# Gate rows and output of the text tokens merged into one 32-column tiled run, text adds moved to GpSimd, first P copy moved to VectorE

## The chip, the cores and the metric

The kernel runs on one core of one Trainium2 chip. A core has TensorE (matrix products into the accumulator memory PSUM), VectorE, ScalarE and GpSimd for elementwise work, and DMA queues that are issued from SyncE (SP), ScalarE (ACT) and GpSimd (POOL). In the profile they are PE (with PEld for the loading of a product's stationary operand), DVE, ACT, POOL and SP. The time is the device's time of one execution in microseconds (us); a kernel's time is the median of several.

## The reference

One attention block in which image and text tokens attend jointly. Batch B is 2, with 256 image tokens and 32 text tokens each, width D = 1152; all inputs are bfloat16.

```python
mod_i = (_silu(c) @ wmod_img).reshape(B, 6, 1, D)
mod_t = (_silu(c) @ wmod_txt).reshape(B, 6, 1, D)
shi, sci, gai = mod_i[:, 0], mod_i[:, 1], mod_i[:, 2]
sht, sct, gat = mod_t[:, 0], mod_t[:, 1], mod_t[:, 2]
hi = _layernorm(x_img) * (1 + sci) + shi
ht = _layernorm(x_txt) * (1 + sct) + sht
qkvi, qkvt = hi @ wqkv_img, ht @ wqkv_txt
q, k, v = (concatenate([text part, image part], axis=1) for each third)
p = softmax(einsum('bqd,bkd->bqk', q, k) * D ** (-0.5))
a = einsum('bqk,bkd->bqd', p, v)
at, ai = a[:, :Nt], a[:, Nt:]
out_i = x_img + gai * (ai @ wo_img)
out_t = x_txt + gat * (at @ wo_txt)
```

The change touches the probabilities p, the text gate gat and the text output out_t.

## The kernel before

Width D is cut into KT = 9 row blocks of 128. All products go through the helper `mm` (line 61), transposes through `tr` (line 64); both pin their instruction into program order on TensorE with `pin` (`tc.keep_in_program_order`, line 58). VectorE and ScalarE instructions that are not pinned are placed by the tile scheduler. Every PSUM tile comes from one of two pools: `ps_mm` (six buffers) and `ps_tr` (two buffers, lines 55 and 56). The pool `work` (line 53) has two buffers per tag; the tag "tmp" holds an output product before the residual is added.

Weights lie in five large slots (`wtile`, line 76) that are reused. They are all loaded from the SP queue, one after the other, in the order of the calls; a load waits until the last reader of its slot is done. The end of that order is lines 566 to 571: text key weights, image gate weights, text value weights, image output weights `w_o_i`, text gate weights `w_ga_t`, and last the text output weights `w_o_t`. `load_rows` (line 93) cuts a load into pieces of whole row blocks; `w_o_t` comes in blocks 0 to 4 and 5 to 8. It takes the slot of the text value weights, so its load is issued when `v_txt(1)` (line 696) has read them.

The end of the kernel, in TensorE's order:

1. Scores and softmax (lines 672 to 693), the image gate rows, and the text values `v_txt` (line 505). `v_txt` and `mod_rows` (line 525) use a narrow form: TensorE is cut into four strips of 32 columns, `tile_position=(0, 32 * g)`, and four products run side by side.
2. The transposed probabilities: `p_transposes` (line 630) makes three PSUM tiles, one per block of keys; `p_out` (line 638) copies them to pT in SBUF, in halves for the two batch elements.
3. Attention, `attn_pair` (line 657), three times; the first products read the first half of the first P tile.
4. `out_img(i, ...)` (line 708) for the four image token tiles of 128 tokens. A tile is done in column chunks of CH = 384 (the last tile in 384, 384, 224 and 160): nine products of 128x128 by 128x384 fill a PSUM tile, VectorE multiplies it by the image gate `gb` into a tmp buffer (line 721), adds the input x_i (line 722), and a DMA stores the row.
5. `txt_gate` (line 556) is called by `out_img(1)` after its first chunk. `mod_rows` makes the 36 gate products, ScalarE copies them (line 535), and GpSimd's queue writes the two batch rows to a scratch in memory (line 537) and reads them back spread over the token partitions into `gbf` (line 561), four DMAs.
6. `out_txt` (line 728) stands between `out_img(2)` and `out_img(3)`. The 64 text tokens of both batch elements are one stationary operand of 64 columns; two products run side by side in two 64-column strips. Two PSUM tiles (r = 0, 1), 18 products each; VectorE multiplies each by gbf (line 738) and adds the text input xf (line 739); two stores go out on the SP and ACT queues.

Of the kernel before, what the change touches and what calls it, by code (L numbers as in the profile page):

```python
# [14 lines left out]
def kernel(  # L15
# [14 lines left out]
    nc = tc.nc  # L30
    bf = mybir.dt.bfloat16
    f32 = mybir.dt.float32
    PSUM = bass.MemoryType.PSUM

    B, NI, D = x_img.shape
    NT = x_txt.shape[1]
    P = 128
    KT = D // P
# [3 lines left out]
    NTT = B * NT  # L42
    CH = 384
    NCH = D // CH
    VC = 288
# [9 lines left out]
    ps_mm = ctx.enter_context(tc.tile_pool(name="ps_mm", bufs=6, space=PSUM))  # L55
    ps_tr = ctx.enter_context(tc.tile_pool(name="ps_tr", bufs=2, space=PSUM))

    pin = tc.keep_in_program_order

    def mm(*a, **k):  # L60
        return pin(nc.tensor.matmul(*a, **k))  # L61

    def tr(*a, **k):
        return pin(nc.tensor.transpose(*a, **k))  # L64
# [6 lines left out]
    x_i = act.tile([P, NIT, D], bf)  # L71
# [4 lines left out]
    def wtile(slot):  # L76
        return wpool.tile([P, KT, D], bf, tag="w%d" % slot, name="t")

    def wview(src, c0):
        return src.rearrange("(kt p) n -> p kt n", p=P)[:, :, c0:c0 + D]  # L80
# [3 lines left out]
    def load_w(slot, src, c0, splits=(D,)):  # L84
        t = wtile(slot)
        sv = wview(src, c0)
        o = 0
        for n in splits:
            nc.sync.dma_start(t[:, :, o:o + n], sv[:, :, o:o + n])
            o += n  # L90
        return t

    def load_rows(slot, src, c0, cuts=(0, 3, 6)):
        t = wtile(slot)
        sv = wview(src, c0)
        for r0, r1 in zip(cuts, cuts[1:] + (KT,)):
            nc.sync.dma_start(t[:, r0:r1, :], sv[:, r0:r1, :])
        return t
# [147 lines left out]
    def x_tiles(k0, b):  # L246
        return (tp61 if b else tp60) if k0 == 6 else ps_tr.tile([P, 3, NI], bf, tag="tr", name="tp")
# [70 lines left out]
    t3, t0, t6 = [(x_tiles(k0, 1), k0, 1) for k0 in (3, 0, 6)]  # L318
# [63 lines left out]
    def qk_img(wq, blk, hooks):  # L382
        for j in range(KT):
            for hook in hooks.get(j, ()):
                hook()
            ps = ps_mm.tile([P, B * NI], f32, tag="mm")
            for kt in range(KT):
                mm(ps[:], lhsT=wq[:, kt, j * P:(j + 1) * P], rhs=hT_i[:, kt, :],
                   start=(kt == 0), stop=(kt == KT - 1))
            qk_evac(qkT[:, blk * KT + j, :, 0:NI], ps[:].rearrange("p (b n) -> p b n", b=B), blk)  # L390
# [51 lines left out]
    def shift_part(r0, r1):  # L442
        def run():
            for kt in range(r0, r1):
                for b in range(B):
                    acc, col = acc_sh[:, b, :], sTf[:, kt, b:b + 1]
                    if kt == 0:
                        pin(nc.vector.tensor_scalar(acc, w_sh_t[:, kt, :], col, None, op0=ALU.mult))
                    else:
                        pin(nc.vector.scalar_tensor_tensor(acc, w_sh_t[:, kt, :], col, acc,  # L450
                                                           op0=ALU.mult, op1=ALU.add))
        return run
# [62 lines left out]
    def v_txt_out(r, ps):  # L515
        pin(nc.vector.tensor_sub(v_t[:, r * VC:(r + 1) * VC], ps[:], svb[:, r * VC:(r + 1) * VC]))
        if r == 0:
            pin(nc.vector.tensor_sub(v_t[0:NTT, HD:HD + NTT], ps[NTT:P, 0:NTT], svb[NTT:P, 0:NTT]))
# [6 lines left out]
    def mod_rows(w_blk):  # L525
        gps = ps_mm.tile([P, VC], f32, tag="mm")
        for kt in range(KT):
            for g in range(NGG):
                mm(gps[32 * g:32 * g + 32, :], lhsT=sT32[:, kt, :], rhs=w_blk[:, kt, g * VC:(g + 1) * VC],
                   start=(kt == 0), stop=(kt == KT - 1), tile_position=(0, 32 * g))  # L530
        return gps

    def mod_row_out(gps, si):
        g_sb = work.tile([P, VC], bf, tag="garow")
        pin(nc.scalar.copy(g_sb[:], gps[:]))
        for b in range(B):
            nc.gpsimd.dma_start(gsc[si, b, :].rearrange("(g j) -> g j", g=NGG), g_sb[b:P:32, :])

    gb = act.tile([P, B, D], bf, tag="Bt")
    gbf = act.tile([P, 2, VC], bf)  # L540
    xf = act.tile([P, 2, VC], bf)
# [14 lines left out]
    def txt_gate():  # L556
        mod_row_out(mod_rows(w_ga_t), 1)
        for g in range(2):
            for b in range(B):
                r0 = 64 * g + 32 * b  # L560
                nc.gpsimd.dma_start(gbf[r0:r0 + NT, :, :],
                                    gsc[1, b, :].rearrange("(r g j) -> g r j", r=2, g=2)[g].partition_broadcast(NT))
# [5 lines left out]
    w_v_t = load_w(1, wqkv_txt, 2 * D)  # L568
    w_o_i = load_rows(4, wo_img, 0)
    w_ga_t = load_w(3, wmod_txt, 2 * D)  # L570
    w_o_t = load_rows(1, wo_txt, 0, (0, 5))
    qk_img(w_q_i, 0, {0: (shift_part(0, 2),), 3: (txt_stats, shift_part(2, 4), txt_var, txt_norm),
                      5: (shift_part(4, 7),), 8: (shift_part(7, KT),)})
    qk_img(w_k_i, 1, {1: (txt_transposes,), 4: (txt_rows_scale, shift_blocks, txt_scale),
# [3 lines left out]
    aT = act.tile([P, KT, B * NTOK], bf, tag="Q")  # L578
# [51 lines left out]
    def p_transposes(kj, pool):  # L630
        ps = pool.tile([P, B * NTOK], bf, tag="tr" if pool is ps_tr else "mm", name="pT_ps")
        k0 = kj * P
        for pb, c0, o in [(pbs[(0, qi)], k0, qpos[0][qi]) for qi in range(TPB)] + [(pbs["t"], k0, NI)] + \
                [(pbs[(1, qi)], k0 - (NT if kj == 2 else 0), NTOK + qpos[1][qi]) for qi in range(TPB)]:
            tr(ps[:, o:o + P], pb[:, c0:c0 + P], ident[:])
        return ps

    def p_out(kj, ps, copy, b0=0, b1=B):
        pin(copy(pT[:, kj, b0 * NTOK:b1 * NTOK], ps[:, b0 * NTOK:b1 * NTOK]))
# [55 lines left out]
    v_txt_out(0, vt[0])  # L695
    vt.append(v_txt(1))
    pt0, pt1, pt2 = p_transposes(0, ps_tr), p_transposes(1, ps_tr), p_transposes(2, ps_mm)
    v_txt_out(1, vt[1])
    p_out(0, pt0, nc.scalar.copy, 0, 1)
    p_out(0, pt0, nc.vector.tensor_copy, 1, B)  # L700
    p_out(1, pt1, nc.scalar.copy, 0, 1)
    p_out(2, pt2, nc.vector.tensor_copy)
    p_out(1, pt1, nc.scalar.copy, 1, B)
    img_gate_spread()
    for dts in ((0, 5, 1), (6, 2, 7), (3, 8, 4)):
        attn_pair(*[[(b, dt) for dt in dts] for b in range(B)])

    def out_img(i, chunks, parts=None, between=None):
        b = i // TPB
        t0 = b * NTOK + qpos[b][i % TPB]  # L710
        o = work.tile([P, D], bf, tag="o")
        c0 = s0 = 0
        for n in chunks:
            if c0 and between:
                between = between()
            ps = ps_mm.tile([P, CH], f32, tag="mm")
            for dt in range(KT):
                mm(ps[:, 0:n], lhsT=aT[:, dt, t0:t0 + P], rhs=w_o_i[:, dt, c0:c0 + n],
                   start=(dt == 0), stop=(dt == KT - 1))
            tmp = work.tile([P, CH], bf, tag="tmp")  # L720
            nc.vector.tensor_mul(tmp[:, 0:n], ps[:, 0:n], gb[:, b, c0:c0 + n])  # L721
            nc.vector.tensor_add(o[:, c0:c0 + n], tmp[:, 0:n], x_i[:, i, c0:c0 + n])  # L722
            c0 += n
            if parts is None and c0 == D or parts and c0 in parts:
                (nc.scalar if parts and c0 == D else nc.sync).dma_start(oi_v[b, i % TPB, :, s0:c0], o[:, s0:c0])
                s0 = c0

    def out_txt():
        of = work.tile([P, 2, VC], bf, tag="of", bufs=1)
        for r in range(2):  # L730
            ps = ps_mm.tile([P, VC], f32, tag="mm")
            for dt in range(KT):
                for g in range(2):
                    c0 = (2 * r + g) * VC
                    mm(ps[64 * g:64 * g + NTT, :], lhsT=aT[:, dt, NI:NI + NTT], rhs=w_o_t[:, dt, c0:c0 + VC],
                       start=(dt == 0), stop=(dt == KT - 1), tile_position=(0, 64 * g))
            tmp = work.tile([P, CH], bf, tag="tmp")
            nc.vector.tensor_mul(tmp[:, 0:VC], ps[:], gbf[:, r, :])
            nc.vector.tensor_add(of[:, r, :], tmp[:, 0:VC], xf[:, r, :])
        for g in range(2):  # L740
            eng = nc.sync if g == 0 else nc.scalar
            eng.dma_start(ot_flat.rearrange("t (r g j) -> g t r j", r=2, g=2)[g], of[64 * g:64 * g + NTT, :, :])

    C3 = (CH, CH, CH)
    out_img(0, C3)
    out_img(1, C3, between=txt_gate)
    out_img(2, C3)
    out_txt()
    out_img(3, (CH, CH, 224, 160), parts=(2 * CH, D - 160, D))


# [28 lines left out]
```

## Time and profile before

| | us |
|---|---|
| median of 5 runs (lowest, highest) | 117.51 (117.22, 117.61) |
| the profiled execution | 117.67 |
| its span, first to last instruction | 115.5 |
| TensorE busy | 109.8 |
| VectorE busy | 72.1 |
| ScalarE busy | 43.7 |
| GpSimd busy | 12.1 |
| mean DMA rate over the span | 355 GB/s |

The granted clock of TensorE is 1.0 throughout. The profile's timeline merges instructions of one line and one kind: a row has the start, the time covered, the engine, line, operation, tiles, the shapes, the count, and in brackets the idle time before with what ended it. "PEld" rows show when TensorE changes to other stationary operands; their starts mark the stages. SPq, ACTq and the POOL DMA rows are the issue of DMAs, and the landing is given apart. A duration of a TensorE product includes its pipeline; products that follow each other start closer together than that.

### The profile page before, as it was taken

The page shows a single profiled execution, that of the slowest core. Times are in us where ns is not written, and L with a number is a line of the kernel's source. Part 1 is how long each engine was busy: PE and PEld are TensorE (multiplying, and loading weights), DVE is VectorE, ACT ScalarE, POOL GpSimd, SP SyncE. Part 2 cuts the span into 40 slices and gives each one's busy share as a digit, 9 for nine tenths or more (in the row PEclk, how much of TensorE's full clock was granted, in tenths as well). Part 3 has the DMA queues.
Part 4 walks back from the last instruction along what each step waited for, and adds up shares of the span by engine and source line. Part 5 has one row for each costly group of instructions (what it writes and reads, how often), then busy time and mean ns, then how long its engine had stood idle before and what let it go on. Part 6 is the DMA issues. An engine that isn't in the chain of part 4 may idle for free.

```text
span 115.5 us, 2579 instructions
## 1 busy us (share of the span) xinstructions
PE 109.8 (95%) x1078; PEld 63.4 (55%) x1078; DVE 72.1 (62%) x152; ACT 43.7 (38%) x93; POOL 12.1 (11%) x32
## 2 busy tenths in 40 slices
PE   4988999999999999999999999999999999999990
PEld 2335644445574444445444458787866556656670
DVE  3569592063869999999996040018768509566571
ACT  5799700041752279825240324244647400100000
POOL 7200000000000000000000000002440700415000
PEclk9999999999999999999999999999999999999999
DMA  3999999999999999999999999999999999942223
GB/s 118 372 361 389 397 403 409 415 412 409 410 400 413 335 402 407 406 415 410 413 366 386 413 404 413 409 411 406 412 404 410 404 419 367 397 180 51 102 51 102
DMA packets 18917, 41.02 MB, mean 355 GB/s; under 512 B 1323, under 2 KB 1851, under 8 KB 18907
## 3 DMA queue, kind: packets, MB, share of 16 engines
q1 hardware_dynamic: 18032, 39.85, 89.8%
q0 software_dynamic: 480, 0.89, 2.4%
q10 hardware_dynamic: 395, 0.12, 0.4%
q8 instruction: 8, 0.13, 0.4%
q14 instruction: 2, 0.02, 0.0%
HBM read 39.52 MB, written 1.34 MB: 354 GB/s over the span
## 4 chain that ended last, share of the span: by engine, by line
PE 86%; ACT 5%; DMA 3%; DVE 3%; issue 1%; DVEq 0%
PE ps L61 53%; PE vps L61 15%; PE gps L61 5%; PE aps L61 5%; PE sps L61 4%; DMA x_i<-in_x_img_dram 3%; ACT xn_i L194 2%; ACT xn_i L195 2%; PE tp L64 1%; DVE tmp L721 1%; PE pT_ps L64 1%; PE sc_ps L61 1%; DVE o L722 1%; DVE xT_i L257 0%; DVE xn_i L209 0%
## 5 line engine op out<-in xcount | busy, mean ns | idle before, releaser
L61 PE MATMUL ps<-xT_i,t 128*128 128x512 bf16 x162 | 35.7, 379 | 0.0
L61 PEld LDWEIGHTS <-t 128*128 128x128 bf16 x333 | 21.0, 98 | 19.3 <-issue 0.7
L450 DVE SCALAR_TENSOR_TENSOR acc_sh<-t,sTf,acc_sh 128x1152 f32<-128x1152 bf16 x16 | 21.4, 1405 | 0.0
L61 PE MATMUL ps<-t,aT 128*128 128x384 bf16 (+3 forms) x153 | 20.3, 308 | 0.0
L61 PE MATMUL vps<-t,hS_i 128*128 128x512 bf16 (+1 forms) x108 | 17.9, 326 | 0.2 <-DVE hS_i L269 0.2
L61 PEld LDWEIGHTS <-aT 128*128 128x128 bf16 (+1 forms) x153 | 13.0, 101 | 7.1 <-issue 0.8
L61 PEld LDWEIGHTS <-hS_i 128*128 128x128 bf16 x108 | 9.1, 98 | 8.9 <-DVE hS_i L269 0.4
L721 DVE TENSOR_TENSOR tmp<-ps,gb 128x384 bf16<-128x384 f32 (+2 forms) x13 | 6.8, 525 | 7.8 <-PE ps L61 7.8
L380 ACT CAST qkT<-ps 128x512 bf16<-128x512 f32 (+2 forms) x11 | 6.1, 552 | 14.8 <-PE ps L61 13.5
L607 POOL TENSOR_SCALAR pb<-e,rs 128x32 bf16<-128x32 f32 (+1 forms) x5 | 2.3, 458 | 76.1 <-DVE rs L599 76.1
L378 ACT ACTIVATE qkT<-ps 128x512 bf16<-128x512 f32 (+2 forms) x11 | 5.9, 559 | 8.2 <-PE ps L61 8.2
L177 DVE CAST v_i<-vps 128x512 bf16<-128x512 f32 x5 | 3.5, 692 | 8.0 <-PE vps L61 8.0
L61 PE MATMUL wps<-warm 128*128 128x512 bf16 x24 | 7.0, 446 | 1.5 <-DVE unit L127 1.5
L587 DVE TENSOR_REDUCE nmx<-sps 128x1 f32<-128x288 f32 x4 | 1.8, 458 | 9.4 <-PE sps L61 9.4
L179 ACT CAST v_i<-vps 128x512 bf16<-128x512 f32 x4 | 2.3, 580 | 10.2 <-PE vps L61 10.2
L61 PEld LDWEIGHTS <-sT 128*32 128x32 bf16 x180 | 4.5, 96 | 1.8 <-issue 1.2
L61 PE MATMUL sps<-qkT 128*128 128x288 bf16 (+1 forms) x54 | 5.3, 287 | 0.0
L652 DVE TENSOR_SCALAR aT<-aps,svc 128x288 bf16<-128x288 f32 x9 | 4.3, 518 | 1.5 <-PE aps L61 1.5
L61 PE MATMUL gps<-t,sT 128*32 128x288 bf16 x144 | 5.2, 287 | 0.0
L61 PEld LDWEIGHTS <-warm 128*128 128x128 bf16 x25 | 2.6, 112 | 4.8 <-issue 1.9
L61 PE MATMUL aps<-pT,v_i 128*128 128x288 bf16 x36 | 5.1, 287 | 0.0
L61 PE MATMUL ps<-hT_t,t 128*128 128x64 bf16 x162 | 5.1, 193 | 0.0
(112 smaller groups left out, 104.8 us busy)
## 6 DMA issues: line engine op xcount, KB each, us to landing
t<-in_wqkv_txt_dram SPq DMA_DIRECT2D x3, 2592.0 KB, 19.5
t<-in_wmod_img_dram SPq DMA_DIRECT2D x2, 2592.0 KB, 14.4
t<-in_wmod_txt_dram SPq DMA_DIRECT2D x2, 2592.0 KB, 18.6
t<-in_wqkv_img_dram SPq DMA_DIRECT2D x3, 864.0 KB, 13.5
t<-in_wqkv_img_dram SPq DMA_DIRECT2D x1, 2592.0 KB
t<-in_wo_img_dram SPq DMA_DIRECT2D x3, 864.0 KB, 10.3
t<-in_wqkv_img_dram SPq DMA_DIRECT2D x3, 576.0 KB, 10.9
t<-in_wmod_txt_dram SPq DMA_DIRECT2D x2, 864.0 KB, 13.2
```

The costliest lines, as they stand in the source:

```text
L61: return pin(nc.tensor.matmul(*a, **k))
L64: return pin(nc.tensor.transpose(*a, **k))
L177: nc.vector.tensor_copy(out_ap, in_ap)
L179: nc.scalar.copy(out_ap, in_ap)
L194: pin(nc.scalar.activation(junk, x_ap, ACT.Copy, scale=1.0 / D, accum_out=sm[:, 0:1]))
L195: pin(nc.scalar.activation(junk, x_ap, ACT.Square, scale=float(D) ** -0.5, accum_out=sm[:, 1:2]))
L378: nc.scalar.mul(out_ap, in_ap, SCALE)
L380: nc.scalar.copy(out_ap, in_ap)
L450: pin(nc.vector.scalar_tensor_tensor(acc, w_sh_t[:, kt, :], col, acc, op0=ALU.mult, op1=ALU.add))
L607: pin(nc.gpsimd.tensor_scalar(dst, src, rs[0:qn, :], 0.0, op0=ALU.mult, op1=ALU.add))
L652: nc.vector.tensor_scalar(dst, tiles[(b, dt)][:], bias, None, op0=ALU.add)
L721: nc.vector.tensor_mul(tmp[:, 0:n], ps[:, 0:n], gb[:, b, c0:c0 + n])
```

## The change

- Text gate rows: no longer inside `out_img(1)`, but right behind it.
- Text output products: right behind the gate rows, ahead of `out_img(2)`. They use strips of 32 columns, one batch element and column group per strip: 72 products instead of 36. They first take row blocks 0 to 6 for both tiles, then 7 and 8. The tiles come from `ps_tr` and are held.
- Text output, VectorE part: a function of its own, `out_txt_store`, behind `out_img(2)`. The product stays on VectorE; the add goes to GpSimd. The stores follow it.
- `w_o_t` is loaded as blocks 0 to 6 and 7 to 8.
- VectorE's output operations are pinned in program order. In that order the text products precede the operations of the last image tile, whose first two tmp buffers are the ones that GpSimd's adds read.
- P copies: the first half of the first P tile moves to VectorE, ahead of `v_txt_out(1)`; its second half moves from VectorE to ScalarE, behind ScalarE's first half of the second tile.

```diff
-    w_o_t = load_rows(1, wo_txt, 0, (0, 5))
+    w_o_t = load_rows(1, wo_txt, 0, (0, 7))
...
+    p_out(0, pt0, nc.vector.tensor_copy, 0, 1)
     v_txt_out(1, vt[1])
-    p_out(0, pt0, nc.scalar.copy, 0, 1)
-    p_out(0, pt0, nc.vector.tensor_copy, 1, B)
     p_out(1, pt1, nc.scalar.copy, 0, 1)
+    p_out(0, pt0, nc.scalar.copy, 1, B)
     p_out(2, pt2, nc.vector.tensor_copy)
     p_out(1, pt1, nc.scalar.copy, 1, B)
...
-            if c0 and between:
-                between = between()
...
-            nc.vector.tensor_mul(tmp[:, 0:n], ps[:, 0:n], gb[:, b, c0:c0 + n])
-            nc.vector.tensor_add(o[:, c0:c0 + n], tmp[:, 0:n], x_i[:, i, c0:c0 + n])
+            pin(nc.vector.tensor_mul(tmp[:, 0:n], ps[:, 0:n], gb[:, b, c0:c0 + n]))
+            pin(nc.vector.tensor_add(o[:, c0:c0 + n], tmp[:, 0:n], x_i[:, i, c0:c0 + n]))
...
     def out_txt():
+        tiles = [ps_tr.tile([P, VC], f32, tag="tr", name="txo") for r in range(2)]
+        for d0, d1 in ((0, 7), (7, KT)):
+            for r, ps in enumerate(tiles):
+                for dt in range(d0, d1):
+                    for g in range(2):
+                        for b in range(B):
+                            c0, r0, t0 = (2 * r + g) * VC, 64 * g + NT * b, NI + NT * b
+                            mm(ps[r0:r0 + NT, :], lhsT=aT[:, dt, t0:t0 + NT], rhs=w_o_t[:, dt, c0:c0 + VC],
+                               start=(dt == 0), stop=(dt == KT - 1), tile_position=(0, r0))
+        return tiles
+
+    def out_txt_store(tiles):
         of = work.tile([P, 2, VC], bf, tag="of", bufs=1)
-        for r in range(2):
-            ps = ps_mm.tile([P, VC], f32, tag="mm")
-            for dt in range(KT):
-                for g in range(2):
-                    c0 = (2 * r + g) * VC
-                    mm(ps[64 * g:64 * g + NTT, :], lhsT=aT[:, dt, NI:NI + NTT], rhs=w_o_t[:, dt, c0:c0 + VC],
-                       start=(dt == 0), stop=(dt == KT - 1), tile_position=(0, 64 * g))
+        for r, ps in enumerate(tiles):
             tmp = work.tile([P, CH], bf, tag="tmp")
-            nc.vector.tensor_mul(tmp[:, 0:VC], ps[:], gbf[:, r, :])
-            nc.vector.tensor_add(of[:, r, :], tmp[:, 0:VC], xf[:, r, :])
+            pin(nc.vector.tensor_mul(tmp[:, 0:VC], ps[:], gbf[:, r, :]))
+            pin(nc.gpsimd.tensor_add(of[:, r, :], tmp[:, 0:VC], xf[:, r, :]))
...
     out_img(0, C3)
-    out_img(1, C3, between=txt_gate)
+    out_img(1, C3)
+    txt_gate()
+    txt = out_txt()
     out_img(2, C3)
-    out_txt()
+    out_txt_store(txt)
     out_img(3, (CH, CH, 224, 160), parts=(2 * CH, D - 160, D))
```

More of the change, by code (lines that the diff above doesn't have):

```diff
@@ L706, with out_img @@
         attn_pair(*[[(b, dt) for dt in dts] for b in range(B)])
-    def out_img(i, chunks, parts=None, between=None):
+    def out_img(i, chunks, parts=None):
         b = i // TPB
```

## The prediction

> **What bounds the kernel now.** I read the page first, then the chain that ended last, then the timeline of the last 30 us, because every edit lies there.
>
> ```profile
> PE 109.8 (95%) x1078; PEld 63.4 (55%) x1078; DVE 72.1 (62%) x152; ACT 43.7 (38%) x93; POOL 12.1 (11%) x32
> ```
> TensorE is busy 95% of 115.5 us. The chain, from 78 us on:
> ```profile
> 84.22 0.94 PE pT_ps L64 x15
> 85.17 5.87 PE aps L61 x54
> 91.03 5.85 PE ps L61 x36
> 96.88 1.22 PE gps L61 x36
> 98.10 12.79 PE ps L61 x99
> 110.89 0.02 issue
> 110.91 0.57 DVE tmp L721
> ```
> TensorE carries the end until 110.9 us. From there VectorE does: at 110.91 it takes the second column chunk of the last token tile, and its six operations then run without a gap to 113.0. So two times matter: when the last image tile starts on TensorE (call it F, 107.77 now), and when VectorE starts that second chunk (call it V, 110.91, which is F + 3.14). The timeline, merged rows:
> ```profile
> 96.81 0.98 PEld L61 LDWEIGHTS <-sT 128*32 128x32 bf16 x36 [0.32 <-issue]
> ...
> 98.03 7.10 PEld L61 LDWEIGHTS <-aT 128*128 128x128 bf16 x45 [0.24 <-issue]
> ...
> 98.84 1.22 POOL L537 DMA_DIRECT2D mod_scratch<-g_sb  x2 [7.24 <-ACT g_sb L535]
> ...
> 103.41 2.17 POOL L561 DMA_DIRECT2D gbf<-mod_scratch  x4 [3.36 <-DMA mod_scratch<-g_sb]
> ...
> 105.44 2.10 PEld L61 LDWEIGHTS <-aT 128*64 128x64 bf16 x36 [0.32 <-issue]
> ...
> 107.27 0.46 DVE L738 TENSOR_TENSOR tmp<-ps,gbf 128x288 bf16<-128x288 f32 x1 [0.77 <-DMA gbf<-mod_scratch]
> ...
> 107.77 4.38 PEld L61 LDWEIGHTS <-aT 128*128 128x128 bf16 x36 [0.23 <-issue]
> ...
> 109.45 0.56 DVE L721 TENSOR_TENSOR tmp<-ps,gb 128x384 bf16<-128x384 f32 x1 [0.67 <-PE ps L61]
> ```
> See three things. TensorE leaves its full-width shape twice, for the gate rows (96.81) and for the text output (105.44). The gate rows take a long way round: copy, write to memory, read back (gbf), and VectorE waits for that at 107.27. And VectorE idles 0.67 us before the last tile, so the text work there costs nothing today.
>
> **One tiled run instead of two.** Image matmuls follow each other at 0.1625 us (36 in 6.01 us, less one duration of 0.33, over 35). Four 32-column matmuls take 0.1225 us (the 36 gate matmuls: 1.29 less 0.29 is 1.00 us for eight steps of four). The gate visit spans 96.56 (start of the last image matmul) to 98.03, 1.47 us; less one image step and nine steps of 0.1225 leaves 0.21 for going there and back. The text visit spans 105.19 to 107.77, 2.58; less 0.16 and eighteen steps leaves 0.22. Text now has 72 matmuls in fours, again eighteen steps; the same form exists in the trace (72 text value matmuls in 2.49 us from 81.73), so it gains and loses nothing. Merging saves one visit: 0.22 us.
>
> **The P copies.**
> ```profile
> 84.64 1.00 ACT L639 COPY pT<-pT_ps 128x288 bf16<-128x288 bf16 x3 [1.33 <-PE pT_ps L64]
> ...
> 85.92 0.11 PEld L61 LDWEIGHTS <-v_t 32*128 32x128 bf16 x6 [0.24 <-DVE pT L639]
> ```
> The first attention matmul (85.09) waits for ScalarE's copy (0.40 us from 84.64). VectorE's copy of that shape takes 0.31, so up to 0.09 is gained. But VectorE now does copy, text subtraction and the third copy in a row, 0.31 + 0.46 + 0.45 from 84.65, to 85.87 at most; the text part of attention that needs it starts at 85.92 today. So the gain lies between 0 and 0.09; I take 0.05. ScalarE's two later copies end near 85.95, before their reader at 86.27. No cost.
>
> **The text weights.** Text output moves from 105.44 to right behind the gate rows. Those start 18 image steps later than now less 0.05: 96.81 + 2.93 - 0.05 = 99.69; the text follows 1.11 later, at 100.80. Its weights are the last load in the SP queue:
> ```profile
> t<-in_wo_txt_dram SPq DMA_DIRECT2D x1, 1152.0 KB, 17.5
> ```
> That piece was issued at 84.69, so all nine row blocks are there at 102.2. The new first piece lacks two blocks, 590 KB. At 424 GB/s (the window 99 to 100 us) they take 1.39 us: seven blocks at 100.8. From a landing to the reader's start the trace shows 0.12 us (the last gbf read, issued at 105.05 with 2.1 to landing, and VectorE at 107.27), so the first text matmul runs at 100.95, 0.15 late. Bounds: no wait, or 0.5 if the queue lags by a third of a microsecond. The last two blocks are needed 1.7 us later, at 102.65; they are there. The SP queue is not reordered otherwise; the second tile's store goes out about 1.2 us earlier, behind the weights. All later image work hangs on this: F = 107.77 - 0.22 - 0.05 + 0.15 = 107.65.
>
> **The gate's way round.** The gate rows end 2.87 us later. The second memory write, issued at 99.46 now, is issued at 102.33. Its landing took 3.8 us under full load (rows: 3.8 to 4.9); the nearest quiet rows, the gbf reads, took 2.1 to 2.3. I take 2.2, since the DMA share falls from 1.07 (99 to 100 us) to 0.56 and 0.07 (101 to 103); the moved store fills part of that. Landing at 104.5; today landing (103.28) to VectorE (107.27) is 4.0, so gbf is usable at 108.5. VectorE gets there at T = F + 1.07 = 108.72 (0.20 from the last full-width step, 0.59 for the product, 0.36 for the add, less 0.09 overlap). Hidden, with 0.2 in hand. Fully loaded: 110.1, which is 1.4 too late.
>
> **The adds on GpSimd.** This is the new wait. Only two tmp buffers exist. The text products fill both, and GpSimd's adds free them; the last tile's first product now waits for GpSimd's first add, its second product for the second. No two-operand GpSimd row exists. Nearest: copies of 18 and 96 columns, 0.201 and 0.258, so 0.19 + 0.73 ns per column: 0.40 for 288 columns. With the column cost three times (two reads, a write) it is 0.82. Bounds 0.40 and 0.82; I take 0.78, near the upper, since every row there fetches one operand and this one fetches two.
>
> The trace also shows the two engines hold each other up:
> ```profile
> 78.59 0.37 DVE L601 TENSOR_SCALAR pb<-e,rs 128x288 bf16<-128x288 f32 x1
> ...
> 79.50 0.15 DVE L599 RECIPROCAL rs<-rs 128x1 f32<-128x1 f32 x1
> 79.69 0.37 DVE L601 TENSOR_SCALAR pb<-e,rs 128x288 bf16<-128x288 f32 x1
> ```
> ```profile
> 78.75 0.37 POOL L607 TENSOR_SCALAR pb<-e,rs 128x32 bf16<-128x32 f32 x1 [73.35 <-DVE rs L599]
> 79.75 0.47 POOL L607 TENSOR_SCALAR pb<-e,rs 128x32 bf16<-128x32 f32 x1 [0.63 <-DVE rs L599]
> ```
> GpSimd ends 0.16 us after VectorE in both, though it started 0.16 and 0.06 behind it: it was held. I read the last tile's first add on VectorE (two SBUF operands) as held in turn until GpSimd's second add ends; if it is not, V is 0.15 earlier.
>
> So: first text product at T, 0.46; GpSimd starts 0.10 later (the reciprocal's end at 79.65 to 79.75 above); two adds of 0.78 end at T + 2.12; then VectorE's held add, 0.28 (0.36 less the overlap) until the next start: V = T + 2.40 = 111.12, against 110.91. TensorE alone would allow F + 3.14 = 110.79. Moving the adds takes two of 0.31 off VectorE, but it idles there today. The stores of the text, behind GpSimd's second add, leave near 110.9 and land 2.4 later, before the last image store (113.2 + 1.5).
>
> The Trainium skill speaks against this move: GPSIMD Engine Reference, 3.1 and 4.1, has a two-input add at 2.6 cycles per element and sends elementwise work to VectorE; SBUF — State Buffer, Who interferes with whom, has the shared port as an exclusive lock. An estimate by the first page is 0.62 for 288 elements and 0.81 with the copies' fixed 0.19, which would add 0.06 to the sum.
>
> **Sum.** V moves by +0.21 us: -0.22 visit, -0.05 copies, +0.15 weights, +0.33 GpSimd. The work behind V is unchanged. The profiled execution took 117.67, so 117.88; it lies 0.16 above the median of 117.51, so the forecast is 117.7.
>
> **Rivals.** 0.2% (0.235 us) is about what a measurement can tell.
> - Faster: a GpSimd add of 0.6 or less, unheld, leaves V at F + 3.14; with weights in time F is 107.50 and the total 117.24. For it: GpSimd's copies are short. Against: two operands. 0.15.
> - Slower by GpSimd: from 0.79 per add the total passes +0.235; each further 0.1 costs 0.2. At 0.95, or if VectorE's text product also holds GpSimd (0.36), 118.1. For it: the held rows. 0.22.
> - Slower by the gate's way round: gbf later than 108.7 delays V one for one; 0.03 late is past the limit, full load gives 117.7 + 1.4 = 119.1. Against: the weights are in by 102.2. 0.12.
> - Slower by the text weights: each 0.1 later is 0.1 on everything; a wait of 0.5 gives 118.05. 0.08.
> - Forecast, within 0.2%: 0.43.
>
> **Numbers.** Faster 0.15, same 0.43, slower 0.42. The range goes from the fast case, 117.25, to 118.2, past the GpSimd and weight cases; the full-load case stays out. The forecast's own range is 117.3 to 117.75.
>
> **What would show it.** One gap of weight loads of 0.3 us instead of two, text matmuls near 100.95; gbf landed by 108.5; two GpSimd adds near 0.8 us, and the last tile's VectorE work released by GpSimd instead of TensorE. I am wrong if VectorE waits for gbf, if GpSimd's adds take under 0.6, or if text starts after 101.3.

## The result and the profile after

The changed kernel takes 118.15 us (median of 26 runs) against 117.48 us (45 runs): 0.56% slower, ratio 1.0056 with a 95% interval of 1.004 to 1.0071. Two later sets of the same kernel, each beside the kernel before, gave 1.0015 (0.999 to 1.004) and 1.0039 (1.0011 to 1.0066). The single times of the first set lie between 117.47 and 119.26. The sign is the same in all three sets, but the interval of the second includes no change. Each ratio compares kernels measured together, leaves out the few executions in a slower state, and need not be the quotient of the medians (117.89 against 117.61 in the third set).

The profiled execution took 117.94, with a span of 115.7. The chain that ended last, from the first image output matmul on (start, duration, what):

```profile
90.77 8.78 PE ps L61 x54
99.54 1.25 PE gps L61 x36
100.79 0.02 issue
100.81 0.41 ACT g_sb L535
101.22 0.28 issue
101.50 3.32 DMA mod_scratch<-g_sb
104.82 0.29 issue
105.11 0.48 POOL gbf L561
...
106.73 2.13 DMA gbf<-mod_scratch
...
108.98 0.47 DVE tmp L742
109.45 0.07 issue
109.53 0.74 POOL of L743
110.27 0.02 issue
110.29 0.57 DVE tmp L719
```

Before, the chain stayed on TensorE until 110.9. Now it leaves TensorE at the end of the gate rows, and goes through ScalarE's copy, the write to memory, the read back (gbf), the text product and GpSimd's add into the last image tile. For the last 11 us of matmuls TensorE no longer sets the end. The timeline shows two waits of VectorE:

```profile
100.75 2.39 PE L61 MATMUL txo<-t,aT 128*32 128x288 bf16 x72
...
103.07 8.97 PE L61 MATMUL ps<-t,aT 128*128 128x384 bf16 x63
...
108.26 0.36 DVE L720 TENSOR_TENSOR o<-tmp,x_i 128x384 bf16<-128x384 bf16 x1
108.98 0.82 DVE L742 TENSOR_TENSOR tmp<-txo,gbf 128x288 bf16<-128x288 f32 x2 [0.37 <-DMA gbf<-mod_scratch]
109.53 1.42 POOL L743 TENSOR_TENSOR of<-tmp,xf 128x288 bf16<-128x288 bf16 x2 [2.26 <-DVE tmp L742]
110.29 0.56 DVE L719 TENSOR_TENSOR tmp<-ps,gb 128x384 bf16<-128x384 f32 x1 [0.48 <-POOL of L743]
```

VectorE is idle 0.37 us for gbf, and 0.48 us for GpSimd's first add. The text matmuls run as one block of 72 with a single change of shape behind it.

To compare profiles without the scatter of the kernel's first 80 us, I use the points of the prediction: O, the first image output matmul; F, the first matmul of the last image tile; T, the first text product on VectorE; V, the second product of the last tile on VectorE. The table has all profiles (us; differences of times rounded to 0.01); "text wait" is the time from the last gate matmul to the first text matmul, beyond the 0.12 of a normal step. The times are medians with the ratio to the kernel before in the same comparison.

| kernel | text wait | F - O | T - F | V - F | V - O | time, ratio |
|---|---|---|---|---|---|---|
| before | - | 16.90 | -0.50 | 3.14 | 20.04 | 117.48 |
| changed | 0.15 | 16.87 | 1.51 | 3.69 | 20.56 | 118.15, 1.0056 |
| changed, second set | 0 | 16.69 | 1.68 | 3.85 | 20.54 | 117.84, 1.0015 |
| changed, third set | 0.47 | 17.18 | 1.07 | 3.24 | 20.42 | 117.89, 1.0039 |
| adds on VectorE | 0 | 16.69 | 1.60 | 3.89 | 20.58 | 117.74, 1.0017 |
| own tmp buffers | 0 | 16.68 | 1.73 | 3.82 | 20.50 | 117.91, 1.0029 |
| gate rows early | - | 16.92 | 1.07 | 3.24 | 20.16 | 117.53, 0.9994 |
| P copies alone | - | 16.90 | -0.65 | 3.14 | 20.04 | 117.50, 0.9996 |
| gate on ScalarE's queue | 0 | 16.68 | 1.07 | 3.24 | 19.92 | 117.60, 0.9999 |
| the same, weights cut at 6 | 0 | 16.94 | 1.06 | 3.23 | 20.17 | 117.74, 1.0009 |
| before, gate rows late | - | 16.90 | 0.94 | 3.23 | 20.13 | 117.73, 1.0012 |
| before, adds on GpSimd | - | 16.91 | -0.99 | 3.21 | 20.12 | 117.50, 0.9994 |
| text between chunks | 0.53 | 17.23 | -0.39 | 3.12 | 20.35 | 117.54, 0.9996 |
| the same, adds on GpSimd | 0 | 16.69 | -0.40 | 3.12 | 19.81 | 117.62, 1.0019 |

V - O grew by 0.5 us, 0.44% of the time; the three ratios lie on both sides of that. The first set's 1.0056 is about 0.15 us more than its profile shows, and why is not known.

The third set shows two delays side by side:

```profile
101.50 2.39 PE L61 MATMUL txo<-t,aT 128*32 128x288 bf16 x72 [0.31 <-DMA t<-in_wo_txt_dram]
...
109.29 0.82 DVE L742 TENSOR_TENSOR tmp<-txo,gbf 128x288 bf16<-128x288 f32 x2
```

There the text weights came 0.47 late and TensorE lost that much, yet V - O was even a little smaller. The last read of gbf landed at 109.08, just in time, and VectorE did not wait for it: T - F is 1.07, as in the rows where gbf was early. So TensorE's delay and the gate row's way round run in parallel, and the later of the two sets V. From the start of the gate rows to V it is 11.69 and 11.67 us in the first two profiles and 11.55 in the third.

### The profile page after: what moved, and what is told of

Read it like the earlier page. It is cut to its first block, busy times and chain, and to the rows that moved or that the text cites. A ratio compares the mean times of both kernels' runs of the same rounds, so it can differ in the third digit from the quotient of the medians.

```text
span 115.7 us, 2653 instructions
## 1 busy us (share of the span) xinstructions
PE 110.4 (95%) x1114; PEld 63.6 (55%) x1114; DVE 71.3 (62%) x150; ACT 43.8 (38%) x93; POOL 13.5 (12%) x34
## 4 chain that ended last, share of the span: by engine, by line
PE 76%; DMA 8%; ACT 5%; DVE 4%; POOL 2%; issue 2%; DVEq 0%
PE ps L61 44%; PE vps L61 15%; PE gps L61 5%; PE aps L61 5%; PE sps L61 4%; DMA x_i<-in_x_img_dram 3%; DMA mod_scratch<-g_sb 3%; ACT xn_i L194 2%; ACT xn_i L195 2%; DMA gbf<-mod_scratch 2%; DVE tmp L719 1%; POOL gbf L561 1%; DVE xT_i L257 1%; PE pT_ps L64 1%; DVE o L720 1%
## 5 line engine op out<-in xcount | busy, mean ns | idle before, releaser
L61 PE MATMUL ps<-t,aT 128*128 128x384 bf16 (+2 forms) x117 | 17.9, 314 | 0.0
L61 PE MATMUL wps<-warm 128*128 128x512 bf16 x24 | 8.1, 498 | 1.5 <-DVE unit L127 1.5
```

## The experiments

**1. The adds back on VectorE.**

```diff
-            pin(nc.gpsimd.tensor_add(of[:, r, :], tmp[:, 0:VC], xf[:, r, :]))
+            pin(nc.vector.tensor_add(of[:, r, :], tmp[:, 0:VC], xf[:, r, :]))
```

> The changed kernel with the two text adds back on VectorE, all else kept. Theory A (what costs is that the gate row's way round ends after VectorE is free, and that all text work stands in front of the last image tile): VectorE then does two products and two adds, 1.5 us as in the profile before (107.27 to 108.78), and the last tile's second product starts 2.37 us after the text begins, against 2.18 with GpSimd. Slower than the changed kernel by 0.2 us, about 118.35. Theory B (the adds on GpSimd are what costs, 0.48 us of waiting in the profile after): the wait goes and 0.4 to 0.5 us come back, about 117.7.

117.74 us, ratio 1.0017 (0.9992 to 1.0043). The time looked like theory B, the profile did not: V - O is 20.58, as with GpSimd, and VectorE waits 0.45 us for gbf and then works 1.5 us on the text. Its timeline:

```profile
108.85 0.46 DVE L742 TENSOR_TENSOR tmp<-txo,gbf 128x288 bf16<-128x288 f32 x1 [0.45 <-DMA gbf<-mod_scratch]
109.34 0.31 DVE L743 TENSOR_TENSOR of<-tmp,xf 128x288 bf16<-128x288 bf16 x1
...
111.14 0.55 DVE L719 TENSOR_TENSOR tmp<-ps,gb 128x384 bf16<-128x384 f32 x1
```

From T to V it is 2.29 us here and 2.18 with GpSimd, in one profile each. So in this place the adds on GpSimd are no worse than on VectorE. The second set of the changed kernel (experiment 5) came out at the same ratio, 1.0015, so these times do not tell the two apart.

**2. Two tmp buffers of their own for the text.**

```diff
-            tmp = work.tile([P, CH], bf, tag="tmp")
+            tmp = work.tile([P, VC], bf, tag="tmpt", name="tmpt")
```

> The changed kernel with two tmp buffers of their own for the text products, so that the last image tile no longer waits for GpSimd. If the shared buffers cost, the last tile's first product follows the second text product at once: second product 1.7 us after the text begins instead of 2.18, so 0.48 faster, about 117.7. If GpSimd's adds hold VectorE's two-operand add (as the prediction took it), that add waits until GpSimd's second add ends, 2.0 us after the text begins, the second product starts at 2.27 and nothing is gained, about 118.2. The trace tells: the gap between VectorE's first product and first add of the last tile.

117.91 us, ratio 1.0029 (1.0005 to 1.0052). The wait for GpSimd is gone, and a hold has taken its place:

```profile
109.63 0.82 DVE L742 TENSOR_TENSOR tmpt<-txo,gbf 128x288 bf16<-128x288 f32 x2 [0.57 <-DMA gbf<-mod_scratch]
110.17 1.41 POOL L743 TENSOR_TENSOR of<-tmpt,xf 128x288 bf16<-128x288 bf16 x2 [2.35 <-DVE tmpt L742]
110.36 0.55 DVE L719 TENSOR_TENSOR tmp<-ps,gb 128x384 bf16<-128x384 f32 x1
110.94 0.85 DVE L720 TENSOR_TENSOR o<-tmp,x_i 128x384 bf16<-128x384 bf16 x1
...
111.72 0.54 DVE L719 TENSOR_TENSOR tmp<-ps,gb 128x384 bf16<-128x384 f32 x1
```

VectorE's add of two SBUF operands takes 0.85 us instead of 0.36; GpSimd's second add ends at 111.58, VectorE's add 0.2 later. The products, which read one operand from PSUM, ran beside GpSimd's adds at their usual 0.55. From T to V 2.09 us: 0.09 gained, not 0.48. The Trainium skill, SBUF — State Buffer, Who interferes with whom, has a VectorE instruction with two SBUF inputs contend with a GpSimd instruction that reads SBUF, over a port pair that is an exclusive lock. This run agrees, with 0.85 us against 0.36.

**3. Gate rows back inside the second image tile.**

```diff
-    out_img(1, C3)
-    txt_gate()
+    out_img(1, C3, between=txt_gate)
     txt = out_txt()
```

> The changed kernel with the gate rows back inside the second image tile, so TensorE leaves its full shape twice again (+0.22) but the gate row starts its way round 2.9 us earlier; the text products come 0.1 later than their weights, so the weight wait (0.15) goes. Theory A: VectorE never waits for the gate row, the text begins 0.37 earlier less 0.07 for TensorE: 0.3 faster than the changed kernel, about 117.85. Theory B: the wait for the gate row is not what counts, only the 0.07 is seen: 118.2.

117.53 us, ratio 0.9994 (0.9971 to 1.0017): the loss is gone. Experiments 1 and 2, in the same comparison, gave 1.0017 and 1.0029. By V - O this kernel is 0.40 us ahead of the changed one, more than the 0.3 of theory A. TensorE changes shape twice again (F - O 16.92), but gbf lands at 106.9, VectorE waits for nothing in front of the text, and V - F falls from 3.69 to 3.24:

```profile
108.43 0.81 DVE L744 TENSOR_TENSOR tmp<-txo,gbf 128x288 bf16<-128x288 f32 x2
108.97 1.42 POOL L745 TENSOR_TENSOR of<-tmp,xf 128x288 bf16<-128x288 bf16 x2 [3.60 <-DVE tmp L744]
109.73 0.56 DVE L721 TENSOR_TENSOR tmp<-ps,gb 128x384 bf16<-128x384 f32 x1 [0.48 <-POOL of L745]
```

The wait for GpSimd is still 0.48 here, and the kernel is as fast as before: that wait was not the loss.

**4. The P copies alone, on the kernel before.** 
```diff
+    p_out(0, pt0, nc.vector.tensor_copy, 0, 1)
     v_txt_out(1, vt[1])
-    p_out(0, pt0, nc.scalar.copy, 0, 1)
-    p_out(0, pt0, nc.vector.tensor_copy, 1, B)
     p_out(1, pt1, nc.scalar.copy, 0, 1)
+    p_out(0, pt0, nc.scalar.copy, 1, B)
```

> The kernel before with the P copies of the change and nothing else. The prediction's term: 0.05 faster (0 to 0.09), 117.43. Rival: the chain copy, subtraction, third copy on VectorE delays the text part of attention: 0 to 0.1 slower.

117.50 us, ratio 0.9996 (0.9973 to 1.0019). Too small for the clock. In the profiles the first P transpose and O lie 6.71 us apart before, 6.65 here and 6.65 in the changed kernel: 0.06 gained.

**5. The changed kernel again, the gate row on ScalarE's queue, and the weights cut at block 6.** The first is the unchanged kernel. The second has

```diff
-        mod_row_out(mod_rows(w_ga_t), 1)
+        mod_row_out(mod_rows(w_ga_t), 1, nc.scalar)
...
-                nc.gpsimd.dma_start(gbf[r0:r0 + NT, :, :],
+                nc.scalar.dma_start(gbf[r0:r0 + NT, :, :],
```

(`mod_row_out` issues its two writes on the engine it is given), and the third also

```diff
-    w_o_t = load_rows(1, wo_txt, 0, (0, 7))
+    w_o_t = load_rows(1, wo_txt, 0, (0, 6))
...
-        for d0, d1 in ((0, 7), (7, KT)):
+        for d0, d1 in ((0, 6), (6, KT)):
```

> The changed kernel once more, beside the next three on the same chip, because the first run with the adds back on VectorE was faster (117.74) than its profile allows (there the last tile's second product starts 3.89 us after the tile's first matmul, 3.69 in the changed kernel). If the adds on GpSimd cost something that the profiles do not show, this comes out at 118.15 again, 0.4 above it; if the difference was between chips, it comes out near 117.8.

> The changed kernel with the text gate row's writes and reads issued from ScalarE's queue instead of GpSimd's; ScalarE is idle there. Theory A (the gate row's way round is too late): the way gets shorter by the hand-over to GpSimd (0.3) and if the landing is like that of the stores (1.5 to 2.1 against 2.9), gbf is there by 107.7 instead of 108.9, VectorE waits for nothing, and 0.35 to 0.45 us come back: about 117.75. If the landing of the write is held up by the image store and not by the queue, gbf stays late and the time stays: 118.1. Theory B (GpSimd's adds): no change, 118.15.

> The same, and the text output weights cut at block 6 instead of 7, to take away the wait of the first text matmul for its weights (0.15 in the profile after: 0.275 between the last gate matmul and the first text matmul, 0.12 without a wait). If that wait counts, 0.1 to 0.15 less than the run with the ScalarE queue alone, about 117.6; if the three last blocks are then late instead, no change.

The changed kernel: 117.84, 1.0015 (0.999 to 1.004), V - O 20.54 as in the first profile. With ScalarE's queue: 117.60, 0.9999 (0.997 to 1.0029). The trace shows what moved:

```profile
101.18 1.07 ACTq L537 DMA_DIRECT2D mod_scratch<-g_sb  x2
...
103.30 1.76 ACTq L561 DMA_DIRECT2D gbf<-mod_scratch  x4
...
108.30 0.81 DVE L742 TENSOR_TENSOR tmp<-txo,gbf 128x288 bf16<-128x288 f32 x2
```

The reads start at 103.30 instead of 105.11, gbf is complete at 106.5 instead of 108.9, and VectorE has no wait in front of the text. V - F is 3.24 as with the early gate rows, F - O keeps the saved visit (16.68), so V - O is 19.92: 0.62 less than the changed kernel, 0.12 less than before. The times of the two kernels in this comparison, 1.0015 and 0.9999, have overlapping intervals; it is the profile that shows the gain. What follows V was 0.1 longer (4.65 us to the end of the span against 4.55). The last store landed 3.64 us after V in both, so the 0.1 lies behind it; why is not settled.

The cut at block 6 did not help: 117.74, 1.0009 (0.9974 to 1.0044). The first text matmul did not wait, but the text run took longer in the middle, since the last three blocks then came late (TensorE stands 0.26 us in front of them, and they landed at 102.09, 0.05 before it went on); the two timelines:

```profile
100.53 2.38 PE L61 MATMUL txo<-t,aT 128*32 128x288 bf16 x72
```

with the cut at 7, and with the cut at 6

```profile
100.43 2.63 PE L61 MATMUL txo<-t,aT 128*32 128x288 bf16 x72
```

**6. The kernel before with the gate rows late.**

```diff
-    out_img(1, C3, between=txt_gate)
+    out_img(1, C3)
+    txt_gate()
```

> The kernel before with one edit: the gate rows behind the second image tile instead of inside it. Text output, adds, buffers and P copies stay as they were. TensorE does the same work. Theory A: gbf arrives near 109.2 instead of 107.2, VectorE does its 1.5 us of text then, the last tile's second product starts near 111.6 instead of 110.9: 0.6 to 0.7 slower than before, about 118.15. Theory B (GpSimd's adds and their buffers make the loss): no loss here, 117.5.

117.73 us, ratio 1.0012 (0.9981 to 1.0043): not the 0.6 that I expected. VectorE does wait for gbf, 2.21 us:

```profile
108.64 0.46 DVE L738 TENSOR_TENSOR tmp<-ps,gbf 128x288 bf16<-128x288 f32 x1 [2.21 <-DMA gbf<-mod_scratch]
...
110.93 0.55 DVE L721 TENSOR_TENSOR tmp<-ps,gb 128x384 bf16<-128x384 f32 x1
```

Two things make it cheap. The text begins at F + 0.94, and V needs it by F + 0.85 (3.14 less the 2.29 from T to V); the wait fills time in which VectorE had nothing to do. And the write landed faster, 2.19 us after its second issue (102.30 to 104.49) against 2.86 in the changed kernel. I had reckoned with gbf at 109.2; it was there at 108.5. So a late gate row costs only what reaches past F + 0.85. In the changed kernel it does for two reasons: F comes earlier (the saved visit), and the write took longer.

**7. The kernel before with the adds on GpSimd.** 
```diff
-            nc.vector.tensor_add(of[:, r, :], tmp[:, 0:VC], xf[:, r, :])
+            nc.gpsimd.tensor_add(of[:, r, :], tmp[:, 0:VC], xf[:, r, :])
```

> The kernel before with the two text adds on GpSimd and nothing else. There VectorE begins the text 0.5 us ahead of the last tile's first matmul (107.27 against 107.77), so even the second GpSimd add (two of 0.73) ends near 109.3, ahead of the last tile's products at 109.45 and 110.91. If the adds cost only through a late text, nothing changes: 117.5, and the last tile's second product still starts 3.14 us after the tile's first matmul. If GpSimd's adds have a price of their own: 0.2 to 0.5 slower.

117.50 us, ratio 0.9994 (0.9974 to 1.0014). GpSimd's adds, 0.73 us each, end at 108.9, before the last tile's first product; they cost nothing where the text comes early. V - F is 3.21; the 0.07 more lie on TensorE, whose matmuls release VectorE at both points.

**8. The text between the second and third chunk of the third tile, and the changed kernel for the third time.** To the kernel with ScalarE's queue:

```diff
-        for n in chunks:
+        for k, n in enumerate(chunks):
+            if k == 2 and between:
+                between()
...
-    out_img(2, C3)
-    out_txt_store(txt)
+    out_img(2, C3, between=lambda: out_txt_store(txt))
```

once with the adds on VectorE, once on GpSimd with the buffers of experiment 2.

> The changed kernel with the gate row's round on ScalarE's queue, the text products and adds both on VectorE, and these placed between the second and third column chunk of the third image tile instead of behind the tile. With that queue gbf landed 0.7 us before the last tile's first matmul. The text (1.5 us) then delays the third chunk's product by about 0.9 us, but the last tile's second product only needs VectorE 3.14 us after the tile's first matmul, where it is free again: the whole cost of the text goes, and the last tile is set by TensorE alone. From the last tiles' start on as in the kernel before, with one visit to the narrow shape less: 0.2 less than the kernel before, about 117.3. If gbf lands later than the chunk boundary, the wait stands inside the third tile and eats the slack: 117.5 to 117.7.

> The same place and queue, but with the adds on GpSimd and two tmp buffers of their own for the text. VectorE's add of the third chunk is held until GpSimd's second add ends (in the run with buffers of their own it took 0.85 us instead of 0.36), about 2.0 us after the text begins; the last tile's first product is then some 0.2 to 0.5 late, and its second is still in time. As the run with the adds on VectorE, within 0.1: 117.3 to 117.4. If the hold reaches the last tile's second product: 0.2 more.

> The changed kernel for the third time, beside these three. Its two sets gave ratios of 1.0056 and 1.0015 to the kernel before. The profiles put the loss at 0.5 us from the first image output matmul to the last tile's second product (20.56 and 20.54 against 20.04), which is 0.4%: 118.0.

The adds on VectorE: 117.54, 0.9996 (0.997 to 1.0022). On GpSimd: 117.62, 1.0019 (0.9996 to 1.0042). The changed kernel beside them: 117.89, 1.0039 (1.0011 to 1.0066). In both, V - F is down to 3.12, TensorE's own pace. But in the first profile the text weights came late, and TensorE paid:

```profile
101.41 2.39 PE L61 MATMUL txo<-t,aT 128*32 128x288 bf16 x72 [0.36 <-DMA t<-in_wo_txt_dram]
```

The second had no such wait and reached V - O = 19.81, the lowest of all, 0.23 below the kernel before; its VectorE add was again held to 0.85 us, in a place where it does no harm:

```profile
107.84 1.42 POOL L745 TENSOR_TENSOR of<-tmpt,xf 128x288 bf16<-128x288 bf16 x2 [15.97 <-DVE tmpt L744]
108.03 0.55 DVE L721 TENSOR_TENSOR tmp<-ps,gb 128x384 bf16<-128x384 f32 x1
108.62 0.85 DVE L722 TENSOR_TENSOR o<-tmp,x_i 128x384 bf16<-128x384 bf16 x1
```

The tail behind V is 0.1 longer in both. No version is measurably faster than the kernel before.

The spans of all executions bear the cause out. Against the kernel before, the mean span is longer by 0.24 and 0.37 us in the second and third set of the changed kernel and by 0.16 and 0.25 in experiments 1 and 2, all with the late gate row on GpSimd's queue. With the gate rows early it is 0.05 shorter, and in the four kernels with ScalarE's queue it is within 0.02 of the kernel before. One such difference is uncertain by about 0.2, but the two groups do not overlap.

## Why the prediction was right or wrong

The time, 118.15, lies inside the range, near its upper end. The likeliest case, no change within 0.2%, did not come; "slower", given 0.42, did. That it lies inside the range is in part luck: the upper end was drawn for the GpSimd and weight cases, and the loss came mainly by the gate row, which the prediction had called hidden. By its steps:

- **The merged run, -0.22.** Right. F - O is 16.90 before and 16.68 to 16.69 where nothing waits for weights.
- **The P copies, -0.05.** Right, 0.06 by the profiles; the times cannot show it.
- **The text weights, +0.15.** The first profile has just this 0.15, but that is one draw. Over nine profiles of the merged order with the cut at 7 or 6 the first text matmul waited in three, 0.15, 0.47 and 0.53, and in six not at all. The upper bound of 0.5 was needed. In the third set a wait of 0.47 alone would have brought nearly the whole loss, with or without the gate row. Its profiled execution, 119.19, was the longest of its twelve, so how often such a wait comes is open.
- **The gate's way round, "hidden, with 0.2 in hand".** This step failed. I took the quiet rows' 2.2 us for the write's landing; it took 2.86 (2.69 to 2.94 in four more profiles with GpSimd's queue and this order). This profile runs 0.2 ahead of the one before (first P transpose at 83.95 against 84.16), so the forecast 108.5 for gbf means 108.3 here; VectorE's text began at 108.98, and the 0.7 is the landing. VectorE could have begun at F + 1.07 = 108.54, as forecast (108.72 less 0.2). Moving the gate rows early or putting them on ScalarE's queue takes V - F from 3.69 to 3.24: 0.45 us. The rival had named the mechanism, the place and the price ("delays V one for one"), with a chance of 0.12, which was too low for a step with 0.2 us of slack and a landing bounded between 2.1 and 3.8.
- **The adds on GpSimd, +0.33.** The size of one add was near (0.73 measured, 0.78 taken; the estimate from the Trainium skill, GPSIMD Engine Reference, 3.1, was 0.81). The hold exists, as experiment 2 shows. But the term was too large: with gbf in time V - F is 3.24, 0.10 over TensorE's 3.14. The last tile's first product waits for the first add anyway, and by the time VectorE reaches the two-operand add, GpSimd's second add is nearly over (110.94 against 110.88): the hold has next to nothing left to hold, and that add took its usual 0.36. Nor is the 0.10 a price of GpSimd: with VectorE's adds, 2.29 from T to V, an estimate by the same T - F of 1.07 gives 3.36. It is what the text costs in front of the last tile.
- **The sum.** From the first P transpose to V, the profiles give 26.75 before and 27.21 after: +0.46 against +0.21. It is -0.06, -0.22, +0.19 (F - O of 16.87 against 16.68), +0.10 and +0.45. The terms are good to 0.02. The two errors, gate row and GpSimd, had opposite signs.

What the prediction missed in its way of counting: it treated the saved visit as a gain, whatever else happened. Once the chain runs through memory, the matmuls' 0.22 us only make VectorE wait longer for gbf.

Left open: why the write lands later in the merged order. In the trace its last completion trails: 15 of the 16 of the second write are in by 103.87, the last comes at 104.97; in experiment 6 they are in by 104.00 and the last comes at 104.49. The image store issued ahead of it shows the same straggler (103.47, then 104.67). Experiment 6 has the old cut of the weights and the same straggler in its store (102.97, then 104.10), so the new cut is not needed for it. From ScalarE's queue (experiment 5) the store trails too (103.09, then 104.24), but the two writes have five completions each instead of 16, and are in by 103.46. What makes the straggler was not tried.

## What to carry to other kernels

Before moving a producer later, follow its result to the last consumer, round trips through memory included, and compare the arrival with the latest time at which that consumer's engine can start without delaying what it does next; slack smaller than the spread of the DMA landings is no slack. A matmul saving in front of such a round trip is worth nothing while the round trip ends later. Elementwise work for GpSimd cost nothing here where it came early (experiment 7); beside it, a VectorE add with two SBUF operands was held until GpSimd was done, with buffers of its own too (experiments 2 and 8).

## What the runs showed of the hardware that was not expected

A VectorE add of two SBUF operands stretched from 0.36 to 0.85 us beside GpSimd's adds, twice, while VectorE's products with a PSUM operand kept 0.55. GpSimd's add of two 128x288 bfloat16 operands took 0.73 us in every profile (0.723 to 0.729 in the first). The same write and read of the gate row from ScalarE's queue were issued 1.6 to 2.1 us apart in four profiles, against 3.4 to 3.7 us from GpSimd's in five, in the same place of the kernel.
